# Two V tiles, memsets and two rows moved out of the preparation, zero products in the backward loop, and later transfers and row sums in the forward loop

## The chip, the cores and the metric

The kernel runs on one core of one Trainium2 chip. The metric is the device time of one execution in microseconds (us); before the change it was 2558.02 us in the median of three runs (2557.34 to 2561.41). Every ratio below is of runs in the fast state on the same chip and in the same rounds. Stage times are compared across chips as well. The profile of a run is one execution, so figures by stage are single observations unless several runs are named.

PE is TensorE, ACT is ScalarE, DVE is VectorE, POOL is GpSimd, SP is SyncE, which here only issues transfers. A "half-clock window" is a stretch in which the profile shows TensorE at clock 0.50; in the trace of before, the 45 such stretches between 1130 and 2440 us start on one grid of 3.413 us, and each is one step of it long or a multiple. A "pair" is two successive blocks of the backward loop: one with PE transposes and one without.

## The reference, cut to what matters

A transformer block with conditioned layer norms: attention of 32 heads of 16 dimensions over 2048 tokens, then a dense part with a squared ReLU; all gradients are returned beside the output.

```python
h = layernorm(x) * (1 + ca) + sa
x = x + ga * attention(h, wqkv, wo)            # softmax(q k^T / 4) v, B=1, S=2048, H=32, Dh=16
h = layernorm(x) * (1 + cb) + sb
x = x + gb * (relu(h @ w1 + b1) ** 2 @ w2 + b2)
# out_0 = x; out_1..out_9 = gradients for x, wqkv, wo, w1, b1, w2, b2, c, w_mod
```

## The kernel before

The program has a preparation (layer norm, first keys and queries, first V tiles), a forward attention loop of 512 units with the dense part of finished chunks woven in, a last dense chunk, a backward loop, and a tail. The backward loop works on groups of four heads, eight of them, each 16 blocks or 8 pairs long. I call the seven places where one group follows another *head changes*. A block has four units; a unit is 128 queries by 512 keys by four heads.

A unit's dS (128 x 2048 bf16, 0.524 MB) has to be transposed for the dQ product. Seven of the eight units of a pair are transposed by a DMA on SyncE's queue, the eighth by TensorE with two copies on ScalarE, the "dsT copies" by which I time the pairs:

```python
def on_pe(b):
    return b % 2 == 1

def transpose_unit(u):
    hg, kc, qc, qi = units[u]
    if qi == 0:
        dqt[u // 4] = tpool.tile([P, 4, 16, P], BF, name="dsT", tag="dsT")
    if qi == 3 and on_pe(u // 4):
        return
    SP.dma_start(out=dqt[u // 4][:, qi], in_=bst[u][1].rearrange("p h k -> p (h k)"), transpose=True)

def pe_turn(b, half):                       # tokens t1, t2; T1, T2 are its two copies on ScalarE
    pt = psx.tile([P, 8, P], BF, name="ptT", tag="px")
    for i in range(8):
        kt = i % 4
        PE.transpose(pt[:, i, :], held["dS"][:, 2 * half + i // 4, kt * P:(kt + 1) * P], identb[:])
    ...
order_t = (                                  # s score, e exponential, D dP and dS, q dK/dV products, d dQ products
    "s0 s1 q s2 e0 e1 D s3 D e2 s4 e3 t1 e4 q T1 D "
    "s5 s6 e5 t2 e6 s7 T2 e7 D s8 e8 D s9 e9 q q s10 "
    "s11 e10 D d1 d2 e11 Q q s12 D e12 s13 e13 q s14 D e14 "
    "s15 q q e15 ").split(), "ABCABBABACABABCA"   # the PSUM bank of each score; ptT and the dQ sums share bank C
```

Loads of the next group's rows and stores of finished gradients are issued from ScalarE, between its exponentials:

```python
def load(to, fro):
    ACT.dma_start(out=to, in_=fro)

def plan_head(hg):
    j0 = (hg - 1) * 128 + 14
    loads = list(kvq_loads(hg)) + list(row_loads(hsets[hg % 2]["do"], dOT_st, hg, slice(0, n), d_st))
    for i, (to, fro) in enumerate(loads):
        at(j0 + 4 * i, load, to, fro)
    at(j0 + 40, spread_qz, hg)
# in dq_out, at the end of a group:
    for hq in range(4):
        r = hg % 2 * 64 + hq * DH
        at(cur["j"] + 6 + hq, load, dQc[hg // 2, r:r + DH, :], st["dq"][32 * hq:32 * hq + DH, :])
```

In the forward loop the woven dense part fetches w2 in slices (through the same queue as a store and a transpose), and GpSimd sums rows of g twelve units after their load:

```python
later(3, sp, dx1_st[:, ts, :], dx1_c)
daT = cb.tile([P, 4, DC, P], BF, name="daT", tag="T4")
later(3, sp, daT.rearrange("p t o q -> p (t o) q"), flat(da_c), True)
w2_nat = load_wB(w2_src, 1, 0.67)
...
later(12, sums)
```

Of the kernel before, what the change touches and what calls it, by code (L numbers as in the profile page):

```python
# [34 lines left out]
def kernel(  # L35
# [111 lines left out]
    with ExitStack() as ph:  # L147
# [142 lines left out]
        def chunk_loads(c):  # L290
            ts = slice(4 * c, 4 * c + 4)
            end = c == QC - 1
            if end:
                L = dict(begun)
            else:
                L = {"w1": load_wA(w1_src, 6), "w1T": load_wB(w1T_st[:], 20)}
                L["g"] = cb.tile([P, 4, D], BF, name="g_c", tag="g_c")
                sp(L["g"][:], g_dram[:, ts, :])
            L["wo"] = ffw.tile([P, DC, D], BF, name="wo_nat", tag="wo")
            sp(L["wo"][:], A_wo.rearrange("(oc p) j -> p oc j", p=P))  # L300
            L["x1"] = cb.tile([P, 4, D], BF, name="x1_c", tag="x1_c")
            sp(L["x1"][:], x_dram[:, ts, :])
            L["gf"] = cb.tile([P, 4, D], BF, name="gf_c", tag="gf")
            L["gfT"] = cb.tile([P, 4, DC, P], BF, name="gfT", tag="gfT")

            def scaled():
                POOL.tensor_tensor(L["gf"][:], L["g"][:], gb_bc.unsqueeze(1).to_broadcast([P, 4, D]), ALU.mult)
                later(6, sp, L["gfT"].rearrange("p t o q -> p (t o) q"), flat(L["gf"]), True)

            def sums():  # L310
                for ti in range(4):
                    rowsum(4, L["g"][:, ti, :], 4 * c + ti)

            if end:
                return L
            later(5, scaled)
            later(12, sums)
            return L

        def dense_chunk(c, O_c, L):  # L320
# [156 lines left out]
            later(3, sp, dx1_st[:, ts, :], dx1_c)  # L477
            daT = cb.tile([P, 4, DC, P], BF, name="daT", tag="T4")
            later(3, sp, daT.rearrange("p t o q -> p (t o) q"), flat(da_c), True)

            w2_nat = load_wB(w2_src, 1, 0.67)
# [183 lines left out]
        def later_stage(i):  # L665
# [34 lines left out]
            if i in (18, 20, 21, 24):  # L700
# [5 lines left out]
                DVE.tensor_tensor(hr, hr, ca1_bc.unsqueeze(1).to_broadcast([P, 4, D]), ALU.mult)  # L706
                DVE.tensor_tensor(hr, hr, sa_bc.unsqueeze(1).to_broadcast([P, 4, D]), ALU.add)
                later(3, sp, h1_st[:, 4 * g:4 * g + 4, :], hr)
# [64 lines left out]
        def normed1(g):  # L773
# [5 lines left out]
            for ti in range(4):  # L779
                t = 4 * g + ti  # L780
                if ti % 2:
# [63 lines left out]
        def prep():  # L845
# [84 lines left out]
            for g in range(QC):  # L930
# [9 lines left out]
                if g > 0:  # L940
                    square(sq[:, g - 1, :], KTs[0][:, chunk_cols(g - 1)])
                keep_warm(4)
# [8 lines left out]
                if g > 0:  # L951
                    norms(g - 1)
# [24 lines left out]
            for t in range(4):  # L977
                value_tile(t, acc4()[:])
            POOL.memset(kts[1][:], 1.0)
            POOL.memset(qts[1][:], 0.0)  # L980
            POOL.tensor_copy(crows[:, 0, :], cbf)
            POOL.tensor_tensor(crows[:, 2, :], crows[:, 0, :], crows[:, 1, :], ALU.mult)
            sp(rows_st[6:9, :].unsqueeze(0), crows)
            run_due(True)

        plan = {}

        def plan_tasks():
# [92 lines left out]
            for t in range(4, TT):  # L1081
                at(t - 4, lambda t=t: value_tile(t, mm()[:]))
            for b, units in ((1, (12, 13, 15, 17)), (2, (23, 24, 26, 28)), (3, (32, 35, 37, 39))):
                for g, u in enumerate(units):
                    at(u, key_tile, b, g)
            for b, units in ((0, (43, 45, 47, 49)), (1, (14, 16, 18, 20)), (2, (25, 27, 29, 31)), (3, (34, 36, 38, 40))):
# [4 lines left out]
            for hb, u in ((1, 19), (2, 30), (3, 33)):  # L1091
                at(u, query_tile, 0, hb)
            for g in range(QC):
                at(42 + 2 * g, query_tile, 1, g)
                at(58 + 2 * g, query_tile, 2, g)
                at(73 + 2 * g, query_tile, 3, g)
                at(52 + 2 * g - (g == 3), token_tile, 0, 0, g)
                at(59 + 2 * g, token_tile, 0, 1, g)
                at((69, 71, 74, 76)[g], token_tile, 0, 2, g)
                at(81 + g, token_tile, 0, 3, g)  # L1100
                for ti in range(4):
                    at(85 + 4 * g + ti, token_tile, 1, g, ti)
            query_bound(21, 0, (1,), 2)
            at(22, b1_turn)
            query_bound(41, 0, (2, 3), 1)
            query_bound(50, 1, (0, 1, 2, 3), 1)
            query_bound(66, 2, (0, 1, 2, 3), 1)
            query_bound(80, 3, (0, 1, 2, 3), 1)
            for j in range(3):
                at(51 + 2 * j, mod_rows, j)  # L1110
                at(56 + j, lambda j=j + 3: sp(wmod_slice(j), wmod_v[:, :, j * D:(j + 1) * D]))
                at(68 + 2 * j, mod_rows, j + 3)
            at(67, lambda: mod_cols_of(mm(), 3, 2))
# [37 lines left out]
        with ExitStack() as ph2:  # L1151
# [3 lines left out]
            with tc.manual_schedule(engines={PE.engine, ACT.engine, DVE.engine, SP.engine, POOL.engine}):  # L1155
                fh[0, 0] = (qts[0], kts[0])
                for u in range(NF + 2):
# [10 lines left out]
                    if u % 4 == 0 and 18 <= u // 4 < 32:  # L1168
                        turn_weights(u // 4 - 18)
# [379 lines left out]
    with ExitStack() as ph:  # L1549
# [81 lines left out]

        def pe_turn(b, half):
# [43 lines left out]
        def dq_out(b):  # L1676
# [22 lines left out]
            "s5 s6 e5 t2 e6 s7 T2 e7 D s8 e8 D s9 e9 q q s10 "  # L1699
# [12 lines left out]
        with tc.manual_schedule(engines={PE.engine, ACT.engine, DVE.engine, SP.engine, POOL.engine}):  # L1712
            head_fill(1)
            POOL.memset(qz[1][:], 0.0)
            nD, nq = -1, -4
            for b in range(NU // 4 + 3):
                toks, bank = order_t if on_pe(b - 1) else order_n
                for tok in toks:
# [5 lines left out]
                    elif c == "e" and b < NU // 4:  # L1724
                        expo(4 * b + i // 4, i % 4)
                    elif c == "D":
# [9 lines left out]
                    elif c == "q":  # L1736
                        if 0 <= nq < 2 * NU:
                            (v_quad if nq % 2 else k_quad)(nq // 2)
                        nq += 1
                    elif c == "t" and 0 <= b - 1 < NU // 4:  # L1740
# [294 lines left out]
```

## Time and profile before

| stage of the profiled run (span 2559.2) | us |
|---|---|
| preparation, to the first forward exponential | 42.7 |
| forward loop, first to last exponential | 971.3 |
| last dense chunk | 120.2 |
| first backward exponential to the first dsT copy | 23.2 |
| backward loop, first to last pair (63 pairs) | 1268.0 |
| tail | 133.7 |

The prediction shows the page's rows for ScalarE and the clock, and the chain. Two rows of the same page matter as well, and the prediction did not use them. They have the mean busy share of the 16 DMA engines in each of 40 slices (64 us each), in tenths, and the GB/s that they moved:

```profile
DMA  7477454356648666979999999999999999999972
GB/s 205 131 192 175 147 129 120 87 166 143 90 94 188 129 141 123 275 199 191 197 196 195 193 199 202 193 197 190 194 200 195 196 197 203 195 199 207 200 243 74
```

The reader is to see that through the whole backward loop (slices 18 to 37, counted from 0) the DMA engines stand at 9 and the rate at 190 to 207 GB/s without a dip. In figures, for 500 us in the middle of that loop (busy time of each engine, then granted clock, the DMA's packet time as a share of 16 engines, which can pass 1, and GB/s):

```profile
1500.00:2000.00 500.00, 462.34 (x4347) 139.98 (x4344) 457.43 (x396) 475.78 (x902) 53.86 (x39) 0.93 1.15 196
```

(In views of busy time the engines stand in the order PE, its weight loads, DVE, ACT, POOL, each with its number of instructions, then granted clock, the DMA's packet time as a share of 16 engines, which can pass 1, and GB/s.) ScalarE has 475.78 of 500 us, the clock is 0.93, and the DMA column is 1.15. The waits of the backward loop before the change, with total, number and longest, name the two gaps that the change fills; the second view is of the forward loop:

```profile
PE psS_C L1595 <- ACT dsT L1744: 28.9, 61, 0.6
PE ptT L1636 <- ACT dsT L1744: 25.9, 60, 0.4
```

```profile
ACT ET L562 <- PE psST L560: 29.1, 21, 8.3
```

### The profile page before, as it was taken

The numbers are of one execution on the slowest core, as the hardware profiler recorded it, in microseconds if no ns is written. First come the engines' busy times: TensorE is split into PE (matmuls) and PEld (weight loads), VectorE is DVE, ScalarE is ACT, GpSimd is POOL, SyncE is SP. The second block draws the span as 40 slices with busy tenths as digits, with TensorE's granted clock in tenths as the row PEclk, the third lists the DMA queues.
The fourth block names the chain that finished last, engine by engine and source line by source line (L and its number), as shares of the span: only waits on it lengthen the run. The fifth ranks groups of instructions, "written<-read, shape, count | busy, mean of one in ns | idle before, by whom it ended". The sixth has DMA issues, their size and how long they took to land.

```text
span 2559.2 us, 50017 instructions
## 1 busy us (share of the span) xinstructions
PE 2327.6 (91%) x18734; PEld 763.9 (30%) x18734; DVE 1814.4 (71%) x2317; ACT 2307.8 (90%) x3577; POOL 347.0 (14%) x370
## 2 busy tenths in 40 slices
PE   8898799989988998999999999999999999999899
PEld 3232223223322323532222222222222222222343
DVE  6655153464435454678998999999999998998862
ACT  7999999999989999549999999999999999999942
POOL 2000101211323141110101101011010110100100
PEclk9999999999999999998999999999999999999999
DMA  7477454356648666979999999999999999999972
GB/s 205 131 192 175 147 129 120 87 166 143 90 94 188 129 141 123 275 199 191 197 196 195 193 199 202 193 197 190 194 200 195 196 197 203 195 199 207 200 243 74
DMA packets 1227128, 447.18 MB, mean 175 GB/s; under 512 B 1103095, under 2 KB 1197751, under 8 KB 1226630
## 3 DMA queue, kind: packets, MB, share of 16 engines
q1 hardware_dynamic: 1198966, 409.14, 81.2%
q0 software_dynamic: 10944, 16.78, 4.6%
q10 hardware_dynamic: 16976, 18.07, 2.6%
q8 instruction: 147, 2.41, 0.4%
q14 instruction: 95, 0.78, 0.1%
HBM read 96.75 MB, written 73.95 MB: 67 GB/s over the span
## 4 chain that ended last, share of the span: by engine, by line
PE 45%; ACT 36%; DVE 7%; issue 7%; DMA 3%; SPq 1%; ACTq 0%; DVEq 0%; POOL 0%
ACT E_u L1601 20%; ACT ET L562 11%; PE dqacc L1673 6%; PE psS_A L1595 4%; PE psST L560 3%; ACT dsT L1744 3%; PE accVK L1646 3%; PE pm L233 3%; PE psS_C L1595 3%; PE psS_B L1595 2%; PE accVK L1655 2%; PE oacc L576 2%; PE pdh L1859 2%; PE pwq L1893 2%; PE pm L398 2%
## 5 line engine op out<-in xcount | busy, mean ns | idle before, releaser
L1615 DVE TENSOR_TENSOR dS_u<-psD_u,E_u 128x1024 bf16<-128x1024 f32 x1024 | 1187.3, 1218 | 105.4 <-PE psS_B L1595 40.8
L562 ACT ACTIVATE ET<-psST 128x1024 bf16<-128x1024 f32 x1024 | 942.6, 1278 | 33.3 <-PE psST L560 32.6
L1601 ACT ACTIVATE E_u<-psS_A 128x512 bf16<-128x512 f32 x768 | 507.9, 661 | 23.3 <-PE psD_u L1613 9.8
L1601 ACT ACTIVATE E_u<-psS_B 128x512 bf16<-128x512 f32 x768 | 503.5, 656 | 5.4 <-PE ptT L1636 1.1
L1613 PE MATMUL psD_u<-iv,ido 32*128 32x512 bf16 x2048 | 423.5, 398 | 2.2 <-DVE dS_u L1615 2.0
L560 PE MATMUL psST<-qt_sb,kt_sb 32*128 32x512 bf16 x2048 | 315.0, 387 | 52.0 <-ACT ET L562 47.6
L1601 ACT ACTIVATE E_u<-psS_C 128x512 bf16<-128x512 f32 x512 | 335.0, 654 | 1.2 <-PE psD_u L1613 0.5
L1595 PE MATMUL psS_A<-ik,iq 32*128 32x512 bf16 x768 | 304.5, 396 | 12.9 <-ACT E_u L1601 2.2
L1595 PE MATMUL psS_B<-ik,iq 32*128 32x512 bf16 x768 | 305.8, 398 | 11.4 <-ACT E_u L1601 4.0
L1646 PE MATMUL accVK<-dS_u,qz 128*32 128x512 bf16 x2048 | 226.7, 414 | 0.3 <-DVE dS_u L1615 0.2
L1595 PE MATMUL psS_C<-ik,iq 32*128 32x512 bf16 x512 | 196.2, 383 | 32.9 <-ACT dsT L1744 28.9
L1595 PEld LDWEIGHTS <-iq 32*128 32x128 bf16 x2048 | 127.6, 91 | 312.0 <-issue 298.4
L1655 PE MATMUL accVK<-E_u,dOs_tok 128*16 128x512 bf16 x2048 | 211.9, 403 | 0.0
L576 PE MATMUL oacc<-ET,vaug 128*32 128x512 bf16 x2048 | 207.5, 395 | 3.2 <-DVE ostage L580 3.2
L1691 POOL TENSOR_TENSOR dQacc<-dQacc,dqtmp 128x512 f32<-128x512 f32 x64 | 81.1, 1268 | 876.8 <-ACT dqtmp L1686 876.8
L1673 PE MATMUL dqacc<-dsT,KS_tok 128*32 128x512 bf16 x2048 | 179.8, 460 | 12.1 <-DMA dsT<-dS_u 2.7
L560 PEld LDWEIGHTS <-kt_sb 32*128 32x128 bf16 x2048 | 84.8, 91 | 340.9 <-issue 320.1
L1744 ACT ACTIVATE dsT<-ptT 128x1024 bf16<-128x1024 bf16 x128 | 148.7, 1162 | 3.3 <-PE ptT L1636 3.0
L251 DVE COPY part<-pm 128x512 f32<-128x512 f32 (+2 forms) x103 | 63.5, 616 | 115.9 <-PE pm L233 110.0
L1613 PEld LDWEIGHTS <-ido 32*128 32x128 bf16 x2048 | 107.0, 91 | 109.7 <-issue 105.3
L1646 PEld LDWEIGHTS <-qz 128*32 128x32 bf16 x2048 | 60.8, 98 | 241.6 <-issue 228.6
L1636 PE MATMUL ptT<-identb,dS_u 128*128 128x128 bf16 x1024 | 80.0, 222 | 32.8 <-ACT dsT L1744 25.9
(403 smaller groups left out, 2391.9 us busy)
## 6 DMA issues: line engine op xcount, KB each, us to landing
p_st<-part POOLq DMA_DIRECT2D x36, 256.0 KB, 5.5
kt_sb<-qkT_st SPq DMA_DIRECT2D x124, 64.0 KB
wA<-in_B_w_dram SPq DMA_DIRECT2D x28, 256.0 KB
dsT<-dS_u SPq DMA_TRANSPOSE x448
wB<-w1T_st SPq DMA_DIRECT2D x21, 256.0 KB
wA<-w2T_st SPq DMA_DIRECT2D x21, 256.0 KB
wB<-in_B_w_dram SPq DMA_DIRECT2D x21, 256.0 KB
p_st<-part POOLq DMA_DIRECT2D x25, 192.0 KB, 4.2
```

The source lines that it names most:

```text
L560: PE.matmul(ps[:, hi, :], kt_sb[r:r + 32, kt * P:(kt + 1) * P], qt_sb[r:r + 32, :], start=True, stop=True, tile_position=(r, 0))
L562: ACT.activation(ET[:, 2 * pair:2 * pair + 2, :], ps[:], AF.Exp, scale=SCALE)
L576: PE.matmul(oacc[32 * hq:32 * hq + 32, :], lhsT, ET[:, hq, :], start=(kt == 0), stop=(kt == TT - 1), tile_position=(0, 32 * hq), skip_grou ...
L1595: PE.matmul(psS[:], st["q"][r:r + 32, qt * P:(qt + 1) * P], st["k"][r:r + 32, kc * 512:kc * 512 + 512], start=True, stop=True, tile_positi ...
L1601: ACT.activation(bst[u][0][:, hq, :], sst.pop((u, hq))[:], AF.Exp, scale=SCALE)
L1613: PE.matmul(psD[:, hi, :], st["do"][r:r + 32, qt * P:(qt + 1) * P], st["v"][r:r + 32, kc * 512:kc * 512 + 512], start=True, stop=True, til ...
L1615: DVE.tensor_tensor(dS_u[:, 2 * pair:2 * pair + 2, :], psD[:], E_u[:, 2 * pair:2 * pair + 2, :], ALU.mult)
L1646: PE.matmul(cur["vk"][32 * hq:32 * hq + 32, :], hst[hg]["qz"][:, qt, hq, :], bst[u][1][:, hq, :], start=(qt == 0), stop=False, tile_positi ...
L1655: PE.matmul(acc[32 * hq:32 * hq + DH, :], dOs_tok[:, qt, (hg * 4 + hq) * DH:(hg * 4 + hq + 1) * DH], E_u[:, hq, :], start=False, stop=(qt ...
L1673: PE.matmul(acc[32 * hq:32 * hq + 32, :], KS_tok[:, kc * 4 + kt, h * DH:h * DH + 32], tT[:, :, hq * 4 + kt, :], start=(kt == 0), stop=(kt ...
L1691: POOL.tensor_tensor(dst2, dst, tmp[:], ALU.add)
L1744: ACT.activation(dst, pt[:], AF.Identity)
```

## The change

The intent has three parts. In the backward loop, "zero products" (a product with a zero block, added to a sum that it doesn't change) fill the gaps in which TensorE waits, so that its clock stays full. In the preparation, work that the first score doesn't need goes into the forward loop. In the forward loop, transfers and row sums move away from what they delayed: in the trace of before the transpose of daT held SyncE's queue for 5.92 us from 719.56, and a product of VectorE that took 0.43 us at 805.30 took 1.37 us at 808.52, beside the row sums. The core of the diff:

```diff
@@ forward loop
-            later(12, sums)
+            later(16, sums)
...
-            later(3, sp, dx1_st[:, ts, :], dx1_c)
+            later(5, sp, dx1_st[:, ts, :], dx1_c)
-            later(3, sp, daT.rearrange("p t o q -> p (t o) q"), flat(da_c), True)
-            w2_nat = load_wB(w2_src, 1, 0.67)
+            later(5, sp, daT.rearrange("p t o q -> p (t o) q"), flat(da_c), True)
+            w2_nat = load_wB(w2_src, 1, 0.5)
...
-                DVE.tensor_tensor(hr, hr, ca1_bc.unsqueeze(1).to_broadcast([P, 4, D]), ALU.mult)
-                DVE.tensor_tensor(hr, hr, sa_bc.unsqueeze(1).to_broadcast([P, 4, D]), ALU.add)
-                later(3, sp, h1_st[:, 4 * g:4 * g + 4, :], hr)
+                later(1, DVE.tensor_tensor, hr, hr, ca1_bc.unsqueeze(1).to_broadcast([P, 4, D]), ALU.mult)
+                later(2, DVE.tensor_tensor, hr, hr, sa_bc.unsqueeze(1).to_broadcast([P, 4, D]), ALU.add)
+                later(4, sp, h1_st[:, 4 * g:4 * g + 4, :], hr)
@@ preparation
-                if ti % 2:
+                if ti == 1:          # one of four normalised tiles on ScalarE
...
+                if g == 3:
+                    norms(2)
-            for t in range(4):
+            for t in range(2):
                 value_tile(t, acc4()[:])
-            POOL.memset(kts[1][:], 1.0)
-            POOL.memset(qts[1][:], 0.0)
-            POOL.tensor_copy(crows[:, 0, :], cbf)
-            POOL.tensor_tensor(crows[:, 2, :], crows[:, 0, :], crows[:, 1, :], ALU.mult)
...
-            for t in range(4, TT):
-                at(t - 4, lambda t=t: value_tile(t, mm()[:]))
+            for t in range(2, TT):
+                at(t - 2, lambda t=t: value_tile(t, mm()[:]))
+            at(2, POOL.memset, kts[1][:], 1.0)
+            at(3, POOL.memset, qts[1][:], 0.0)
+            at(4, psp["silu"])
... (all other tasks of chunk 0 come two units later)
@@ backward loop
+        def keep_warm():
+            PE.matmul(cur["vk"][0:DH, :], KS_tok[:, 0, D:QPAD], dOs_tok[:, 0, :], start=False, stop=False,
+                      tile_position=(0, 0), skip_group_check=True)
-            "s5 s6 e5 t2 e6 s7 T2 e7 D s8 e8 D s9 e9 q q s10 "
+            "s5 s6 e5 f f t2 e6 s7 T2 e7 D s8 e8 D f f s9 e9 q q s10 "
...
+                        if b < 2 and i % 2 == 1:
+                            if nq > 0:
+                                keep_warm()
+                            elif nq < 0:
+                                PE.matmul(idle[:], ones_bf[:], identb.unsqueeze(1).to_broadcast([P, 4, P]), start=True, stop=True)
...
+                    elif c == "f" and 0 < nq < 2 * NU:
+                        keep_warm()
```

## The prediction

> **What bounds the kernel now.** I read the page first, then busy time and granted clock by stage, then the chain that ended last, then timelines of single stretches. The program has five stages: a preparation (to 42 us), the forward attention loop (512 units, to 1015 us), the last dense chunk (to 1133 us), the backward loop (128 blocks of 16 exponentials, to 2428 us) and the tail. In both loops ScalarE is the busiest engine; the page shows it near full from slice 2 on, and exponentials lead the chain:
>
> ```profile
> ACT  7999999999989999549999999999999999999942
> PEclk9999999999999999998999999999999999999999
> ...
> ACT E_u L1601 20%; ACT ET L562 11%; PE dqacc L1673 6%; PE psS_A L1595 4%; PE psST L560 3%; ACT dsT L1744 3%; PE accVK L1646 3%; PE pm L233 3%; PE psS_C L1595 3%; PE psS_B L1595 2%; PE accVK L1655 2%; PE oacc L576 2%; PE pdh L1859 2%; PE pwq L1893 2%; PE pm L398 2%
> ```
>
> The second row is the clue: the TensorE clock is not full. Busy time by 1 us in the backward loop (the column after POOL is the clock) shows what it means:
>
> ```profile
> 1563.00:1564.00 1.00, 0.95 (x9) 0.13 (x8) 0.92 (x2) 1.00 (x3) 0.00 (x0) 0.64 1.12 204
> 1564.00:1565.00 1.00, 1.00 (x12) 0.22 (x12) 0.74 (x1) 0.48 (x2) 0.00 (x0) 0.50 1.14 212
> 1565.00:1566.00 1.00, 1.00 (x12) 0.35 (x12) 0.88 (x1) 1.00 (x2) 0.00 (x0) 0.50 1.10 193
> 1566.00:1567.00 1.00, 1.00 (x16) 0.22 (x8) 0.34 (x1) 0.18 (x2) 0.00 (x0) 0.66 1.17 229
> ```
>
> For 3.4 us the clock is halved, and ScalarE, otherwise at 1.00, falls to 0.48 and 0.18. The same view in 0.5 us steps over the whole run gives 56 such episodes, 44 of them in the backward loop after 1170 us, each of one window of 3.41 us or a multiple. Between the first copies of dsT in successive pairs of blocks I measure 19.1 to 19.3 us without an episode and 20.4 us with one; a few pairs have two (22.3 us). From the first such copy (1157.42) to the last (2425.46) are 1268.0 us for 63 pairs; 63 x 19.25 would be 1212.8. So half-clock windows cost the loop some 55 us, and two more stretches (1136.5 to 1147 and 1150 to 1167.5) cost its start a few.
>
> Why they come is in the PE timeline of one pair: just before them PE waits twice for the copies that free the PSUM bank of its transposes.
>
> ```profile
> 1561.15 0.61 PE L1636 MATMUL ptT<-identb,dS_u 128*128 128x128 bf16 x8 [0.44 <-ACT dsT L1744]
> ...
> 1563.05 0.39 PE L1595 MATMUL psS_C<-ik,iq 32*128 32x512 bf16 x1 [0.47 <-ACT dsT L1744]
> ```
>
> In the forward loop ScalarE is idle for 29 us in all after its first exponential; the timeline names the largest piece, where PE waits for a weight slice and ScalarE for PE:
>
> ```profile
> 733.53 1.01 PE L487 MATMUL pm<-wB,sT 128*128 128x512 bf16 x2 [8.13 <-DMA wB<-in_B_w_dram]
> ...
> 735.18 1.94 ACT L562 ACTIVATE ET<-psST 128x1024 bf16<-128x1024 f32 x2 [8.34 <-PE psST L560]
> ```
>
> [...] the 45 drops between 1130 and 2440 us all start on one grid of 3.4134 us, at clock 0.50. [...] here PE is busy over half of the windows that lead to a drop. [...] a product with the gate row took 0.43 us at 805.30 and 1.37 us at 808.52, when GpSimd ran the four row sums of g (from 808.46). [...]
>
> **An activity count.** I took every warm window of both loops, and summed the streaming time of its products (0.216 us for 512 columns[...]; sixteen V products in 3.68 us agree), weighted by the share of 128 rows that they drive: a score 1/4, a pair 1/2, a quad, a transpose or a zero product 1. This estimate separates the windows almost perfectly: all 53 that led to a drop have at most 1.30 us, all 547 others at least 1.28. If the zero products of the forward loop counted 1/4, 40 windows that kept the clock would fall below the line; so zero products count in full. Slid over a backward pair, the count falls below 1.29 in two places only: windows starting 0.3 us before to 0.7 after the first copy of dsT (lowest 1.11), where nearly all drops lie, and those starting 4.2 to 4.0 us before it (lowest 1.17).
>
> **The change part by part.**
> Backward loop: the instruction lists differ by 266 zero products into accVK and five idle ones. 256 are four in each of the 64 blocks with PE transposes: two before the second transposes, two before the score that waits for the bank, that is in the two waits of 0.44 and 0.47 us shown above. Two products take 0.43 us, so they fit there and lengthen PE's path by 0 to 0.1 us a pair. They lift the count of the bad windows by 4 x 0.216 = 0.86 us, to about 2.0, far over 1.29. The second, narrow place stays: 0.3 of 3.41 us, so about 6 of 64 pairs, at an estimated 0.8 us (before, such a drop cost 0.4; now two of the zero products run at half clock in it), 5 us. Sum: 63 x 19.25 + 5 + up to 6 for the products = about 1221 against 1268: 47 us saved, the first pair's 2.3 us included.
> Start of the loop: 15 products in the first two blocks. The first window (count 0.49) stays cold even with two more (0.9); the later ones (1.14 + 0.6) should keep the clock. Worth 2 us beyond the 2.3.
> Preparation: the first score (42.18 us) waits for the fourth V tile's copy; two tiles fewer are 2 x 0.93 = 1.9 us. The squares' norm for chunk 2 issued earlier takes one of two norm-and-maximum rounds off the end (1.1 us). One of four normalised tiles instead of two on ScalarE, which is full from 13 to 30 us, frees 0.7 us in each of three groups; VectorE takes 0.33 us more, so say 1 us. The memsets and silu rows leave GpSimd while VectorE normalises chunk 3 (two tiles took 2.10 us there, 0.73 elsewhere). Sum 4.5 us; in chunk 0 the moved pieces lie beside exponentials, and every task there comes two units later, which is hidden.
> Forward loop: w2 slices at lags 1 to 4 ahead of the store and transpose (now lag 5): the transpose held the queue for 5.92 us before the last four slices, so the 9.1 us at 735 should go, and 0.8 at 485. Splitting the two 1.23 us products of h1 over units: most of 5.7 us between 199 and 231. Row sums four units later: some 2 of 4.7 us at 810 to 815. The stalls at 320 and 541 to 550 (6.5 us) are untouched. Sum 13 us.
> Together 47 + 2 + 4.5 + 13 = 66.5 us off 2558: **2491 us**.
>
> **Rivals.**
> (1) *Zero products don't count enough, or only move the bad windows.* If the narrow place becomes a lock (a dip that costs 1.2 us makes the pair 20.45 us, almost six windows of 3.413, so the next pair meets the same phase, as the 20.4 us pairs do now), some 20 to 30 of the 47 us come back: 2511 to 2521. For it: the present lock works so. Against: the drop is over before the second two products run, so I find 0.8 us, and a pair of 20.05 us leaves the place at once.
> (2) *PE becomes the bound:* its products are in order, and if the four don't fit the waits, each pair gets up to 0.86 us longer, 55 us in all; gain and cost cancel and the time stays near 2540. Against: both waits end with ScalarE, at 0.44 and 0.47 us.
> (3) *The forward stalls move:* a later transpose or row sum collides elsewhere, or the slices still land late because key loads share the queue; the 13 us become 3, the time 2501.
> (4) *Clock drops were hidden anyway:* then nothing but 18 us comes. Against: pairs with and without differ by 1.1 us each time.
>
> **Range and chances.** If all goes as worked out 2491; rival 3 alone 2501, rival 1 alone 2511 to 2521, both 2525; stalls at the chunk boundaries and head changes that vanish with fewer drops could give another 10 to 15. So 8 in 10: 2474 to 2515. Two per cent is 2506.9: rival 1 in full or rival 2 is needed to miss it; I give these 13%. Slower would take a collision that nothing here shows, 1%.
>
> **What would show it.** Clock by window in the backward loop: a handful of half-clock windows instead of 44, and pairs of 19.2 to 19.4 us. No PE wait over 0.1 us before the second transposes, and ScalarE at 0.99. The first forward score near 37.7 us. No wait for w2 of several us near 730. Many drops starting about 4 us before the first dsT copy would show rival 1; all pairs at 19.8 to 20 us at full clock rival 2; a wait of ScalarE for scores of over 3 us in the forward loop rival 3.

## The result, and the profile after

The changed kernel took 2541.68 us in the median of four runs (2533.73 to 2544.09); the kernel before took 2557.68 in the same rounds. The ratio is 0.9933 with a 95% interval of 0.9905 to 0.9961: the same within 2%. (A ratio is the mean time of one kernel's fast runs over that of the other's fast runs of the same rounds, so it isn't quite the ratio of the medians.) Predicted were 2491 us, 2474 to 2515.

| stage (us) | before | after | mean of four runs of after | after − before, profiled pair | predicted |
|---|---|---|---|---|---|
| preparation | 42.7 | 39.0 | 38.8 | −3.7 | −4.5 |
| forward loop | 971.3 | 970.5 | 964.0 | −0.8 | −13 |
| last dense chunk | 120.2 | 119.4 | 119.6 | −0.8 | 0 |
| first exponential to first dsT copy | 23.2 | 25.5 | 25.5 | +2.3 | −2 |
| backward loop, 63 pairs | 1268.0 | 1252.5 | 1255.4 | −15.5 | −47 |
| tail | 133.7 | 135.3 | 134.4 | +1.6 | 0 |
| sum | 2559.2 | 2542.3 | 2537.6 | −16.9 | −66.5 |

The page after, in the rows that answer to those shown of before:

```profile
ACT  7999999999998999539999999899999999999842
...
PEclk9999999999999999999999999899999999999999
DMA  7476554366649775979999999999999999999972
GB/s 206 128 184 172 164 132 121 87 168 142 92 97 180 134 146 115 275 201 192 196 200 202 197 198 202 201 191 195 205 194 199 196 203 198 201 205 209 200 236 74
...
ACT E_u L1608 22%; ACT ET L562 8%; PE psST L560 4%; PE dqacc L1684 4%; DMA dsT<-dS_u 3%; PE pm L233 3%; PE psS_A L1602 3%; PE oacc L576 2%; PE accVK L1657 2%; ACT dsT L1763 2%; PE psS_B L1602 2%; PE psS_C L1602 2%; PE pdh L1878 2%; PE pm L398 2%; PE pm L412 2%
```

The new entry is "DMA dsT<-dS_u 3%": the transposing DMA has entered the chain that ended last. The GB/s of the backward loop are where they were.

The clock did what was predicted. Busy time by 1 us at the place of a pair that answers to the stretch shown before (from 3.3 us after its first dsT copy; before, from 3.1):

```profile
1553.00:1554.00 1.00, 0.94 (x13) 0.30 (x12) 0.96 (x2) 1.00 (x3) 0.00 (x0) 1.00 1.18 241
1554.00:1555.00 1.00, 0.91 (x20) 0.57 (x20) 1.00 (x2) 1.00 (x3) 0.00 (x0) 1.00 0.71 156
1555.00:1556.00 1.00, 1.00 (x20) 0.20 (x8) 0.62 (x2) 0.85 (x3) 0.00 (x0) 1.00 1.12 213
1556.00:1557.00 1.00, 0.95 (x12) 0.21 (x12) 1.00 (x1) 1.00 (x3) 0.94 (x1) 1.00 1.17 214
```

The clock is 1.00 in each, and ScalarE at 0.85 or more where it had 0.48 and 0.18. The PE timeline of that pair (start, duration, instruction; a wait would stand in brackets):

```profile
1550.36 0.60 PE L1640 MATMUL accVK<-dOs_tok,KS_tok 128*16 128x512 bf16 x2
1550.89 0.62 PE L1647 MATMUL ptT<-identb,dS_u 128*128 128x128 bf16 x8
...
1552.22 0.60 PE L1640 MATMUL accVK<-dOs_tok,KS_tok 128*16 128x512 bf16 x2
1552.76 0.37 PE L1602 MATMUL psS_C<-ik,iq 32*128 32x512 bf16 x1
```

Two zero products stand before the second transposes and two before the score in bank C, and neither has a bracket: the waits of 25.9 and 28.9 us are no longer in the list. Half-clock windows in the backward stage fell from 52 to 20 (after 1170 us, from 44 to 17; I count the time below full clock and divide by the 3.413 us of the grid).

What came in place of the saving shows at the head changes. The seven pairs at the head changes (first pair of each group, by its first dsT copy) took 23.2, 25.3, 25.0, 23.2, 24.0, 21.9 and 20.5 us, 163.1 in all; seven ordinary ones at 19.25 are 134.75. That is 28.4 us more. The other 56 pairs have a mean of 19.45 us. One of the head changes in the timeline of ScalarE (ACTq is its sequencer issuing a transfer):

```profile
1308.55 1.16 ACT L1763 ACTIVATE dsT<-ptT 128x1024 bf16<-128x1024 bf16 x1
...
1309.45 0.74 ACT L1608 ACTIVATE E_u<-psS_B 128x512 bf16<-128x512 f32 x1
...
1310.76 0.32 ACTq L1584 DMA_DIRECT2D dQc<-dQst  x1
...
1311.84 0.74 ACT L1608 ACTIVATE E_u<-psS_A 128x512 bf16<-128x512 f32 x1
1315.07 0.31 ACTq L1584 DMA_DIRECT2D dQc<-dQst  x1
1315.43 0.60 ACT L1608 ACTIVATE E_u<-psS_C 128x512 bf16<-128x512 f32 x1 [2.85 <-DMA dsT<-dS_u]
```

The same place in the chain of waits (start, length, what):

```profile
1309.28 5.77 DMA dsT<-dS_u
...
1315.07 0.31 ACTq L1584
```

And the list of waits of the backward loop after the change has a line that the one of before lacks:

```profile
ACT E_u L1608 <- DMA dsT<-dS_u: 13.0, 5, 3.9
```

A transpose issued at 1309.28 lands 5.77 us later, the third of four dQ stores is held on ScalarE until 1315.07, and the exponentials behind it stand still. The store does not need that transpose's data. In the instructions' operands in the kept trace, the transfers of SyncE and ScalarE share eight semaphores that tell of their landing (101 to 103, 105 to 108 and 110), and this store has the one (110) that the transpose had before it and waits for it: the last update of 110 before the store came at 1315.05 us, and the store was issued at 1315.07. Seven such holds of ScalarE's issues in the loop, of 0.5 to 3.5 us, make 12.6 us. They are where much of the time is lost; why the transposes are late is another question.

ScalarE's waits for transposes, 13.0 us, are not all of the 28.4. Nine of the 17 half-clock windows that are left after 1170 us start inside these seven pairs; after the stall shown, which ends at 1315.43, the clock drops at 1316.54. How the 28.4 us divide between the two was not measured.

SyncE's queue says how it got there. I added up the durations of its 447 transpose instructions in the loop: 1213.5 us (mean 2.715), with 62.3 us between them, about 0.65 us in most pairs or 0.1 us after each. So the queue is occupied but for these small gaps: 7 x (2.715 + 0.1) = 19.7 us a pair, more than ScalarE's 19.25. Before the change the transposes took 1196.2 us with 96.6 us between them; of its 36 pairs of 20.4 to 20.5 us, 21 left the queue 1 to 5 us without one, the other 15 only 0.65 to 0.83 us. So a pair slowed by the clock often left the DMA time to catch up (21 of these 36), but the queue was nearly full before as well.

The same 500 us window after:

```profile
1500.00:2000.00 500.00, 475.43 (x4491) 146.23 (x4488) 462.78 (x400) 478.71 (x910) 54.02 (x40) 0.97 1.16 198
```

Clock 0.93 to 0.97, but ScalarE gains 3 us of 500, and the DMA rate goes from 196 to 198 GB/s.

The forward loop of the profiled run saved only 0.8 us. The stall for w2 at 735 us (8.34 us of ScalarE) became two short ones, which the timelines of PE and ScalarE show as

```profile
728.78 0.59 PE L487 MATMUL pm<-wB,sT 128*128 128x512 bf16 x2 [1.70 <-DMA wB<-in_B_w_dram]
```

```profile
730.33 1.94 ACT L562 ACTIVATE ET<-psST 128x1024 bf16<-128x1024 f32 x2 [1.55 <-PE psST L560]
```

but this run had others, at 192.6 us (4.29 us, for a load of query rows that SyncE issued at 190.07) and at 801.7 us (3.84 us, for a transpose of O that landed 12.8 us after its issue). The totals of ScalarE's waits for scores in the forward loop, in the first run of the changed kernel and in its fourth:

```profile
ACT ET L562 <- PE psST L560: 27.2, 21, 4.3
```

```profile
ACT ET L562 <- PE psST L560: 14.9, 15, 2.3
```

So the forward gain depends on the run: 27.2 us of waits in one, 14.9 in another, 29.1 before. Seventeen traces with the changed kernel's forward code (the four of it and thirteen experiments below) have 955.1 to 970.5 us, with a mean of 962.8; three with the code of before (before, b_products, b_fewer) have 971.3, 972.5 and 974.3, mean 972.7. The part is worth about 10 us, and the profiled run was its worst.

### The profile page after: what moved, and what is told of

Same layout as the page of the kernel before. It is cut to its first block, busy times and chain, and to the rows that moved or that the text cites.

```text
span 2542.3 us, 50562 instructions
## 1 busy us (share of the span) xinstructions
PE 2357.6 (93%) x19003; PEld 778.6 (31%) x19003; DVE 1816.5 (71%) x2321; ACT 2302.1 (91%) x3573; POOL 347.8 (14%) x370
## 2 busy tenths in 40 slices
DMA packets 1227130, 447.21 MB, mean 176 GB/s; under 512 B 1103095, under 2 KB 1197751, under 8 KB 1226630
## 4 chain that ended last, share of the span: by engine, by line
PE 43%; ACT 34%; DVE 8%; issue 7%; DMA 6%; SPq 0%; ACTq 0%; POOL 0%; DVEq 0%; POOLq 0%
ACT E_u L1608 22%; ACT ET L562 8%; PE psST L560 4%; PE dqacc L1684 4%; DMA dsT<-dS_u 3%; PE pm L233 3%; PE psS_A L1602 3%; PE oacc L576 2%; PE accVK L1657 2%; ACT dsT L1763 2%; PE psS_B L1602 2%; PE psS_C L1602 2%; PE pdh L1878 2%; PE pm L398 2%; PE pm L412 2%
## 5 line engine op out<-in xcount | busy, mean ns | idle before, releaser
L1622 DVE TENSOR_TENSOR dS_u<-psD_u,E_u 128x1024 bf16<-128x1024 f32 x1024 | 1186.8, 1216 | 92.2 <-PE psD_u L1620 24.7
L1620 PE MATMUL psD_u<-iv,ido 32*128 32x512 bf16 x2048 | 411.8, 390 | 3.5 <-DVE dS_u L1622 3.3
L1602 PE MATMUL psS_A<-ik,iq 32*128 32x512 bf16 x768 | 295.5, 385 | 14.2 <-ACT E_u L1608 4.0
L1602 PE MATMUL psS_B<-ik,iq 32*128 32x512 bf16 x768 | 296.9, 387 | 8.4 <-ACT E_u L1608 1.1
L1657 PE MATMUL accVK<-dS_u,qz 128*32 128x512 bf16 x2048 | 215.4, 393 | 0.5 <-PE psD_u L1620 0.2
L1666 PE MATMUL accVK<-E_u,dOs_tok 128*16 128x512 bf16 x2048 | 205.3, 390 | 0.0
L1684 PE MATMUL dqacc<-dsT,KS_tok 128*32 128x512 bf16 x2048 | 149.1, 390 | 28.6 <-ACT E_u L1608 13.3
L576 PEld LDWEIGHTS <-vaug 128*32 128x32 bf16 x2048 | 53.1, 93 | 122.6 <-issue 122.6
```

The costliest lines, as they stand in the source:

```text
L576: PE.matmul(oacc[32 * hq:32 * hq + 32, :], lhsT, ET[:, hq, :], start=(kt == 0), stop=(kt == TT - 1), tile_position=(0, 32 * hq), skip_grou ...
L1602: PE.matmul(psS[:], st["q"][r:r + 32, qt * P:(qt + 1) * P], st["k"][r:r + 32, kc * 512:kc * 512 + 512], start=True, stop=True, tile_positi ...
L1620: PE.matmul(psD[:, hi, :], st["do"][r:r + 32, qt * P:(qt + 1) * P], st["v"][r:r + 32, kc * 512:kc * 512 + 512], start=True, stop=True, til ...
L1622: DVE.tensor_tensor(dS_u[:, 2 * pair:2 * pair + 2, :], psD[:], E_u[:, 2 * pair:2 * pair + 2, :], ALU.mult)
L1657: PE.matmul(cur["vk"][32 * hq:32 * hq + 32, :], hst[hg]["qz"][:, qt, hq, :], bst[u][1][:, hq, :], start=(qt == 0), stop=False, tile_positi ...
L1666: PE.matmul(acc[32 * hq:32 * hq + DH, :], dOs_tok[:, qt, (hg * 4 + hq) * DH:(hg * 4 + hq + 1) * DH], E_u[:, hq, :], start=False, stop=(qt ...
```

## The experiments

### Which part of the change does it (b_products, a_noproducts)

b_products is the kernel before with the backward products only; a_noproducts is the changed kernel without them. The edit, added in one and taken out in the other:

```diff
-            "s5 s6 e5 t2 e6 s7 T2 e7 D s8 e8 D s9 e9 q q s10 "
+            "s5 s6 e5 f f t2 e6 s7 T2 e7 D s8 e8 D f f s9 e9 q q s10 "
+   ... keep_warm(), the token f, and the products in the first two blocks
```

In the texts, theory T says that the DMA transposes on SyncE's queue are the limit that takes over; S is the rival that the stores issued at the head change are the cause in themselves. What was expected of b_products:

> The kernel before with the zero products of the backward loop alone. Theory T (the queue that issues the DMA transposes of dS is the new limit: 448 of them at 2.7 us plus 0.1 between, 7 in a pair of blocks, 19.6 us): the half-clock windows fall from 44 to some 12, the loop saves about 15 us, time 2543 (0.994), and the head switches have pairs of 22 to 25 us. If the products were worth the 47 us of the prediction and the rest of the change took 30 back: 2511.

And of a_noproducts:

> The changed kernel without the backward zero products: preparation and forward parts alone. The traces give 3.7 us for the preparation and nothing for the forward loop, so 2554 (0.9985), 44 or so half-clock windows in the backward loop. If the forward parts gave 13 us as predicted: 2541, and then the products gave nothing.

Measured (before 2561.95, seven runs): b_products 2549.25 us, ratio 0.9946 [0.9928, 0.9965]; a_noproducts 2545.69 us, ratio 0.9951 [0.9909, 0.9994]. By stage, b_products has a loop of 1250.8 us with 20 half-clock windows and head changes of 22.8, 24.1, 24.7, 23.4, 23.7, 23.6 and 20.4 us; its forward loop is that of before (972.5). a_noproducts has a loop of 1271.8 us with 51 windows and a forward loop of 961.4. So the products alone make the loop's 17 us and its new head changes, and the rest alone makes the 10 us of the forward loop and the 4 of the preparation. Two expectations were missed: after 1170 us b_products has 17 half-clock windows where some 12 were expected, and a_noproducts gained in the forward loop, where nothing was. The forward and preparation parts have nothing to do with the head changes.

### One transpose fewer, with and without the products (a_fewer, b_fewer)

One of the seven DMA transposes of a pair becomes a memset by GpSimd. The gradient dQ is wrong (relative error 0.208 in out_2); the rest stays right.

```diff
+            if qi == 1 and not on_pe(u // 4):
+                POOL.memset(dqt[u // 4][:, qi], 0.0)
+                return
             SP.dma_start(out=dqt[u // 4][:, qi], in_=bst[u][1].rearrange("p h k -> p (h k)"), transpose=True)
```

> The changed kernel with one of the seven DMA transposes of each pair of blocks replaced by a GpSimd memset (dQ is wrong on purpose). Theory T: the queue needs 6 x 2.8 = 16.8 us of the 19.25, so the pairs stay at 19.25 at the head switches too, the loop saves some 28 us, time 2513 (0.983 of before). Rival S (the stalls at the head switches come from the four stores of dQ in a row, not from a backlog): the stall stays, 2535 to 2541.

a_fewer took 2504.96 us (2499.51 to 2507.96), ratio 0.9773 [0.9751, 0.9796] to before. Head changes are 19.1 to 19.5 us, the loop 1216.9 us, half-clock windows 6. The same edit on the kernel before was expected to do nothing:

> The kernel before with six instead of seven DMA transposes a pair (the seventh a memset by GpSimd; gradient dQ wrong on purpose). Theory T with the clock as a second, separate limit: before, pairs of 20.4 us with a half-clock window were longer than the queue's 19.7, so relieving the queue alone changes little: loop 1258 to 1270 us, time within 10 us of before, still more than 35 half-clock windows in the backward loop. The same edit on the changed kernel took its loop from 1252 to 1217. Rival: the queue alone was the limit before as well, then the loop falls by 30 us or more and the ratio is 0.985 or less.

b_fewer took 2557.90 us, ratio 0.9972 [0.9936, 1.0008], loop 1271.6 us, 52 half-clock windows. Together with the two runs above that is a table of two by two:

| backward loop, us | without zero products | with zero products |
|---|---|---|
| seven DMA transposes a pair | 1268.0 | 1250.8 (b_products), 1252.5 (after) |
| six | 1271.6 | 1216.9 |

Each remedy alone is worth 17 us or nothing; both together are worth 51. The 1216.9 is the prediction's 1221 for this loop. Two limits lie close behind each other, and the prediction had removed one. The 500 us window of a_fewer, then that of b_fewer:

```profile
1500.00:2000.00 500.00, 482.60 (x4654) 148.15 (x4653) 478.11 (x414) 494.47 (x945) 107.37 (x70) 0.99 1.03 177
```

```profile
1500.00:2000.00 500.00, 462.58 (x4341) 139.45 (x4341) 457.76 (x395) 475.33 (x902) 96.05 (x63) 0.93 0.98 170
```

With six transposes and full clock ScalarE reaches 494.47 of 500 us, at 177 GB/s. With the clock of before, the DMA falls to 170 GB/s and ScalarE gains nothing.

### The stores apart (a_spread)

```diff
-                    at(cur["j"] + 6 + hq, load, dQc[hg // 2, r:r + DH, :], ...)
+                    at(cur["j"] + 6 + 8 * hq, load, dQc[hg // 2, r:r + DH, :], ...)
```

> The changed kernel with the four stores of dQ at a head switch eight half-units apart instead of one. Rival S: the stalls of 3 to 6 us at the seven head switches go, 2513. Theory T: the backlog is paid elsewhere (PE or ScalarE then waits for dsT at another place), 2536 to 2542.

It is correct and took 2535.56 us, ratio 0.9889 [0.9866, 0.9913]. The head changes fell to 19.1 to 19.8 us, but the pair after each of the first six rose to 22.2 to 24.9 (after the last, the second pair took 23.0), and the loop took 1252.0 us, as before the edit. The stall follows the stores by one pair, and the loop gains nothing. The time is that of the changed kernel on other chips (2536.5 to 2539.3), so no gain is shown.

### One transpose more (a_extra), with the changed kernel beside it (after_again)

```diff
+            if qi == 1 and not on_pe(u // 4):
+                extra = tpool.tile([P, 16, P], BF, name="dsX", tag="dsX", bufs=1)
+                SP.dma_start(out=extra[:], in_=bst[u][1].rearrange("p h k -> p (h k)"), transpose=True)
```

> The changed kernel with one more DMA transpose of dS per pair of blocks on SyncE's queue (8 instead of 7), into a tile that nothing reads; outputs stay right. Theory T (that queue has no slack: 7 transposes of 2.72 us with 0.1 us between them are 19.7 us a pair, and the loop takes 19.9): every pair gets about 2.8 us longer, 22.5 us a pair, the loop 1420 to 1440 us, the time 2710 to 2730 us, ratio to before about 1.06, and the page names the transpose's DMA as what ScalarE waits for. Rival R (the queue is only late at the change of a head, because of what happens there, and has slack between): the loop stays within 20 us of the changed kernel's, time under 2565.

> The changed kernel once more, unaltered, so that it stands on the same chip as the three below. About 2541 us and 0.993 of before; loop of 63 pairs about 1252 us; forward loop anywhere from 960 to 971 us, since four runs with the same forward code differed by that.

after_again took 2536.88 us, ratio 0.9894 [0.9855, 0.9933], loop 1252.3. a_extra took 2692.76 us, ratio 1.051 [1.0464, 1.0555], loop 1407.9 us. That is 155.6 us for 63 pairs, 2.47 us per added transpose; I had expected 2.8. The rival's "within 20 us" is off the table: an eighth transpose found no slack to hide behind. The 500 us window and two waits of a_extra:

```profile
1500.00:2000.00 500.00, 459.46 (x4035) 134.43 (x4033) 415.56 (x357) 434.59 (x815) 50.06 (x36) 0.88 1.17 200
```

```profile
DVE dS_u L1622 <- DMA dsT<-dS_u: 45.2, 46, 2.5
ACT E_u L1608 <- DMA dsT<-dS_u: 45.0, 16, 5.5
```

The rate is 200 GB/s, hardly more than with seven (198). The miss of 0.3 us per transpose led me to ask for the rate of the DMA engines instead of the queue, since 0.524 MB at 200 GB/s are 2.62 us. By itself this run does not tell the two apart: a queue that costs 2.8 us a piece would need 63 x 8 x 2.8 = 1411 us, and the loop took 1407.9. The next run does.

### The transposes untouched, other transfers taken away (a_noloads)

```diff
-            for i, (to, fro) in enumerate(loads):
+            for i, (to, fro) in enumerate(loads if hg < 2 else []):
                 at(j0 + 4 * i, load, to, fro)
```

Gradients are wrong, since groups 2 to 7 work on old rows.

> The changed kernel without the loads of the next head's rows and tokens inside the backward loop, from the third head group on (stale data instead, gradients wrong on purpose). The transposes are left as they are. Theory D (what the transposes lack is throughput of the DMA engines, which move 198 to 201 GB/s in the loop of before, of the changed kernel and of the one with an eighth transpose alike): about 1.3 MB less per head beside 28 MB of transposes is some 6.5 us of the engines' time per head, more than the backlog of about 5 us, so the head changes after the second fall to 19.3 to 20.5 us, the mean transpose from 2.72 to 2.55 us, the loop from 1252 to about 1225 us, ratio to before about 0.98. Theory Q (each transpose holds SyncE's queue for 2.7 us by its own issue cost, whatever other transfers run): transposes stay at 2.7 us, head changes at 22 to 25 us, loop 1245 to 1255 us.

It took 2512.20 us, ratio 0.9796 [0.9764, 0.9828], loop 1220.1 us. Six head changes are 19.1 to 19.4 us and the last 20.5. The same window shows ScalarE at 495.58 of 500 us and full clock with seven transposes a pair:

```profile
1500.00:2000.00 500.00, 483.38 (x4672) 152.15 (x4669) 478.95 (x415) 495.58 (x947) 61.70 (x44) 1.00 1.15 196
```

The median transpose went from 2.70 to 2.54 us; the mean only to 2.66 where I had said 2.55 (some still are long, and the queue's gaps are 56 us, about as before the edit, so the room is thin). Seven transposes a pair therefore do run at ScalarE's pace when the loads are gone. Theory Q, a cost of the queue by itself, falls; theory D stands: the DMA engines moved 196 to 200 GB/s of this mix in the 500 us windows with seven or eight transposes a pair, and without the later loads the same seven transposes fit into 1220.1 us instead of 1252.3.

The kept traces show the backlog itself. For each unit I take the time from the end of its dS on VectorE to the end of its transpose instruction on SyncE, in the mean of a pair and of the second to seventh group. With the changed kernel it grows from 5.0 us in a group's third pair to 7.3 in its seventh (in its three later traces from 5.0 to 5.8 up to 7.4 to 7.6); in a_noloads it is 6.8 and 6.0, in a_fewer 3.3 and 3.1. One doubt remains about a_noloads alone: it also leaves ScalarE with 72 instead of 204 transfers to issue in the loop, each of which can be held on a shared semaphore, as the store at 1315.07 us was. a_poolst and a_poolq in the next section answer it: no such hold is left in them, and nothing is gained.

The bytes agree. Before, 196 GB/s x 1268.0 us are 248.5 MB in the loop. At the 200 GB/s of a_extra, the most that a window of 500 us showed, they need 1243 us (an estimate from these two numbers); the changed kernel's traces took 1252 to 1260. a_extra's 64 more transposes are 33.6 MB: 282.1 MB by this sum, and 200 x 1407.9 = 281.6 MB by its window. a_noloads moved 196 x 1220.1 = 239.1 MB, which at 200 GB/s would need 1196 us, less than ScalarE's 63 x 19.25 = 1213. The 200 GB/s belong to this traffic, which is nearly all in small packets (before: 1103095 of the run's 1227128 under 512 B); in slice 16 of the page, with other traffic, the rate was 275 GB/s. Whether bytes or packets are what runs out, no run here separates.

### By which wait the lateness is lost (a_poolst, a_poolq, a_poolq_ns, after_third)

The stall at 1315 us suggested a cheap cure: issue stores, or stores and loads, from GpSimd, which in the 500 us window of after was busy for only 54.02 us. (In the trace of after its 76 transfer issues took 0.86 us in the median and 0.90 in the mean, the 0.9 us of the second text below.) a_poolst does it for the stores, a_poolq for both; a_poolq_ns also leaves out the products at the loop's start.

```diff
         def load(to, fro):
-            ACT.dma_start(out=to, in_=fro)
+            POOL.dma_start(out=to, in_=fro)        # a_poolq; in a_poolst for the eight stores of a group only
```

> The changed kernel with the eight stores per head (dQ and dVK) of the backward loop issued by GpSimd instead of ScalarE; the loads stay on ScalarE; outputs stay right. Mechanism W, stores alone: the 2.9 to 4.4 us waits of ScalarE at the head changes go, head changes 19.3 to 21 us, loop 1220 to 1235 us, time 2507 to 2522 us, ratio to before about 0.981. Mechanism W, but loads stall next: loop 1235 to 1250. Mechanism N: head changes stay at 22 to 25 us, loop 1247 to 1257.

> The same with the head loads issued by GpSimd too (some 27 issues of about 0.9 us per head on an engine that is 14% busy); outputs stay right. Mechanism W: ScalarE has no wait on a transfer left in the loop, loop 1218 to 1230 us, time 2505 to 2518 us, ratio to before about 0.980. Mechanism N: loop 1247 to 1257 us, ratio about 0.99.

> The same without the fifteen products in the first two blocks (which cost 4.6 us of start in a_nostart): start 20.9 to 21.5 us instead of 25.5, otherwise like a_poolq, so 4 us less than it; under mechanism W 2501 to 2514 us, ratio to before about 0.978; under N about 2533 us.

> The changed kernel once more, for this chip: 0.989 to 0.993 of before, loop 1250 to 1254 us.

after_third took 2539.32 us (ratio 0.9905 [0.9879, 0.993]), a_poolst 2542.48 (0.9918 [0.9892, 0.9944], loop 1256.4), a_poolq 2552.10 (0.9959 [0.9945, 0.9973], loop 1274.0), a_poolq_ns 2549.54 (0.9951 [0.9931, 0.9971], loop 1269.6). In the texts, mechanism W says that ScalarE's own waits at its issues are the cause and N that they are not. W is refuted: GpSimd's transfers have semaphores of their own (111 to 118 in the trace of after), no issue of ScalarE is held on a transpose by more than 0.3 us in a_poolst, ScalarE issues none in the loop of a_poolq, and neither loop is shorter. (With 1274.0 a_poolq is above N's range too, and a_poolq_ns missed N's 2533.) In a_poolq VectorE has the wait for transposes instead, for the buffer of dS that the transpose still has to read:

```profile
DVE dS_u L1622 <- DMA dsT<-dS_u: 23.9, 22, 4.5
```

Exponentials then wait for scores behind VectorE. In these two runs the late transfers were paid at different waits, ScalarE's 13.0 us in after and VectorE's 23.9 us in a_poolq; moving the issues moved the wait, and the loop got no shorter. Why a_poolq is 17 to 22 us slower in the loop than the changed kernel (1252 to 1257 in the runs up to then) is not settled; it has 30 half-clock windows against 17 to 21.

### Work moved off the DMA (a_relief)

```diff
         def on_pe(b):
-            return b % 2 == 1
+            return b % 2 == 1 or b % 8 == 4
```

> The changed kernel with one unit in every four pairs moved from the DMA queue to PE transposes with two ScalarE copies (every eighth block, besides every second one); outputs stay right. Theory T: 27 transposes of 2.82 us per four pairs are 19.0 us a pair, under ScalarE's 19.25 plus a quarter of the two copies (about 0.3), so no backlog is left: head changes of 19.3 to 20 us, loop 63 x 19.5 to 19.6 = about 1230 us instead of 1252, time about 2520, ratio to before about 0.984 and to the changed kernel about 0.991. Rival R: the head changes keep their 22 to 25 us and the loop gets longer by the copies, about 1262 us.

It is correct and took 2568.11 us, ratio 1.0001 [0.995, 1.0051], loop 1289.2 us. The DMA is relieved, as the window shows:

```profile
1500.00:2000.00 500.00, 474.34 (x4474) 150.46 (x4475) 450.74 (x387) 477.85 (x895) 53.92 (x39) 0.96 1.10 187
```

At 187 GB/s, and with 183 us between SyncE's transposes instead of 56, there is no backlog. But undisturbed groups of four pairs took 80.0 to 80.6 us instead of 4 x 19.25 = 77.0. I had charged the two copies with 1.2 us per moved unit. The timeline above shows 0.90 us from the start of a copy to that of the next exponential, so two are 1.8, and ScalarE stood idle for 14.7 us of the loop just before its copies, nearly all of it for PE's transposes (4.8 in after_again). I mis-sized the price, and the work that left the DMA arrived on the engine that is the other limit.

### The clock: how many products, how many rows (a_two, a_two32)

a_two drops the second "f f"; a_two32 does that and lets each zero product drive 32 rows instead of 128, about as long in time: in the trace of after, the shortest product with 512 columns took 371 ns on 32 rows and 379 ns on 128. In the text on a_two32, "the monitor" is a name for whatever sets the granted clock; the traces show only the clock, at 0.50 or 1.00.

```diff
-            "s5 s6 e5 f f t2 e6 s7 T2 e7 D s8 e8 D f f s9 e9 q q s10 "
+            "s5 s6 e5 f f t2 e6 s7 T2 e7 D s8 e8 D s9 e9 q q s10 "
-            PE.matmul(cur["vk"][0:DH, :], KS_tok[:, 0, D:QPAD], dOs_tok[:, 0, :], ...)
+            PE.matmul(cur["vk"][0:DH, :], KS_tok[0:32, 0, D:QPAD], dOs_tok[0:32, 0, :], ...)   # a_two32 only
```

> The changed kernel with two instead of four zero products in each block with PE transposes (only those before the second transposes); outputs stay right. By the count of the prediction the worst window rises by 0.43 us of full-row products, from 1.11 to 1.54, over the line of 1.29: half-clock windows in the backward loop 15 to 30, as with four (17 to 24), loop 1245 to 1258 us. If two are too few: 35 or more such windows and a loop of about 1268 us.

> The same as a_two, but each zero product drives 32 rows of the array instead of 128; as long in time, outputs stay right. If the monitor counts by rows, as the count of the prediction does, two such products add only 0.11 us, 1.22 in the worst window, under 1.29: half-clock windows stay at 35 or more in the backward loop, the loop at 1262 to 1272 us, ratio to before about 0.997. If it counts time busy, it is like a_two: 15 to 30 windows and a loop of 1245 to 1258 us.

a_two took 2536.75 us, ratio 0.9887 [0.9856, 0.9919], 26 half-clock windows, loop 1255.2: two products do what four do, as the count said. a_two32 took 2548.38 us (ten runs, 2536.92 to 2561.05), ratio 0.9935 [0.9912, 0.9959], with 35 windows and a loop of 1253.8 us in the profiled run, which was the fastest of the ten. The windows are at the edge of "rows count", the loop is not where that theory put it, and the median time lies between a_two and before. Ten of the 35 windows come before 1170 us (3 of a_two's 26), where its start took 29.7 us instead of 25.3; after that it has 25 against 23. The prediction's count, redone on the kept trace of a_two32, decides for the rows as far as one trace can: with the best line for each, 6 of 610 full-clock windows fall on the wrong side when its products count by rows, 11 when they count by time. Why the loop of that run is short stays open.

### The products at the start (a_nostart, a_nostart5, after_fourth)

```diff
-                        if b < 2 and i % 2 == 1:
-                            if nq > 0:
-                                keep_warm()
-                            elif nq < 0:
-                                PE.matmul(idle[:], ones_bf[:], ...)
```

> The changed kernel without the fifteen products in the first two blocks of the backward loop; outputs stay right. From first exponential to first dsT copy: 21 to 23 us instead of 25.5 (the two kernels without them showed 20.9 to 23.2, five with them 24.7 to 25.5), loop unchanged at 1252, time 2 to 4 us less than the changed kernel's 2537 of this chip's last call: ratio to before 0.986 to 0.992. If instead those products are needed against half-clock windows at the start, as the prediction said, the start takes longer than 25.5 us.

> The changed kernel without the fifteen products at the start of the backward loop, five rounds beside the changed kernel: start 20.9 us in the trace, time 3 to 5 us under the changed kernel's of this call (about 0.9985 of it). If the start's gain is given back later in the loop, the two are within 1 us.

> The changed kernel in five rounds on this chip: 0.989 to 0.993 of before, start 25.5 us.

a_nostart took 2533.73 us (ratio 0.9867 [0.9837, 0.9897]). In five rounds on one chip it took 2531.88 us (0.988 [0.986, 0.9901]) beside 2536.50 us of the changed kernel (0.9888 [0.9868, 0.9908]). The start took 20.9 us in both traces, against 25.4 to 25.6 in every run of the changed kernel. It has the lowest median of the versions with right results, 4.6 us under the changed kernel on that chip, though the intervals overlap, so only the stage is shown and the total is likely but not proven.

## Why the prediction was wrong, point by point

- **The clock and its cause: right.** The waits before the second transposes and before bank C went, the half-clock windows fell from 44 to 17 after 1170 us, and a pair without one mostly takes 19.1 to 19.4 us. Of the 17, nine start inside the stalled head-change pairs and five start 0.9 to 1.1 us before a first dsT copy, close to the narrow place to which the prediction gave about six. The count was redone from the trace of before: of 598 full-clock windows (51 led to a drop) the best line, 1.27 us of 3.41, puts 5 on the wrong side, and 24 when the transposes are left out of the count. In 48 of the 51 PE was busy over half of the time. The 0.216 us of the count is in the same trace: of 1524 successive products of 128 rows and 512 columns at full clock, 1297 start 0.215 or 0.216 us after the one before (at clock 0.50, 17 of 23 start 0.426 or 0.427 us after it). Rival 1 (zero products don't count, or a lock) and rival 2 (PE becomes the bound) did not come.
- **The step that failed: "63 x 19.25 + 5 + up to 6 for the products = about 1221 against 1268: 47 us saved".** It takes for granted that the loop runs at ScalarE's pace once the clock is full. It got 15.5 us in the profiled pair of runs. The 56 ordinary pairs are 1089.4 us, 11.4 over 56 x 19.25, about the 5 + 6 that the prediction added. The other 28.4 us are the head changes. The DMA engines moved 196 GB/s in the 500 us window before, 198 after and 200 with an eighth transpose; at 200 the bytes of the loop need about 1243 us (the estimate above). With one transpose fewer the loop took 1216.9 us and without the later loads 1220.1, so the 47 us were there for the clock, but behind a second limit. None of the four rivals named the DMA, although the page of before showed its row at 9 and 190 to 207 GB/s in every slice of that loop. That alone would not have settled it (the row is at 9 in nearly every slice of a_fewer too, which had room), but it was reason to ask.
- **Start of the loop: sign wrong.** "Worth 2 us beyond the 2.3" became a loss: 25.5 us with the products against 20.9 without, 4.6 us. (The kernel before has neither and took 23.2 in one trace, b_fewer 21.2.)
- **Preparation: right.** 42.7 to 39.0 us, 3.7 of the 4.5 predicted (3.9 in the mean of four).
- **Forward loop: right in kind, size by the run.** The 9.1 us for w2 went, as said; other stalls came (rival 3 in part). 0.8 us in the profiled run, about 10 in the mean of seventeen traces against three, 13 predicted. The parts that the prediction lists (9.1, 0.8, most of 5.7, some 2) come to more than its 13.
- **Range and chances: too sure.** A loop that returns 15 where 47 were counted lands some 30 us higher, outside the range, whatever else goes right. "Slower would take a collision that nothing here shows" was fair, but a limit that the page did show was left out of the chances for "same".

## What to carry to other kernels

When a change speeds up one limit of a loop, work out the pace of every other resource in that loop before taking the whole gap as gain; for DMA that is the bytes over the highest rate that a trace shows for the same kind of traffic. Here 249 MB at 200 GB/s left the loop 25 us of the 47. The busy digit did not tell: it stands at 9 in most slices of a_fewer and b_fewer too, at 177 and 170 GB/s, where taking the transpose away had made room. Before the change, 196 GB/s, close to the highest of 200, was a second limit although hardly a wait named it (1.4 us of waits for transposes in the list of waits of that loop), and 21 of the 36 slowed pairs left the queue 1 to 5 us without a transpose; taking traffic away (a_fewer, a_noloads) showed the limit. When a stall moves with a store or its issuing engine and the loop does not get shorter, look for a shortage of throughput behind it: in these runs only less traffic removed it, not another order.
